# Attention over pooled keys followed by a gated feed-forward layer: scores of three batches as split products, four low parts on GpSimd, new orders

## The chip, the core and the metric

One core of a Trainium2 chip runs the whole program. The metric is the device time of one execution in microseconds (us). Of the kernel before, three runs were timed, and one execution was profiled.

## The reference

```python
def _attn_ref(q, k, v):                 # 8 batches, 8 heads, 576 rows, 64 columns
    k_p = k.reshape(B, H, 72, 8, D).mean(axis=3)
    v_p = v.reshape(B, H, 72, 8, D).mean(axis=3)
    scores = scale * np.matmul(q, k_p.transpose(0, 1, 3, 2))
    scores = scores - np.max(scores, axis=-1, keepdims=True)
    attn = np.exp(scores)
    attn = attn / (np.sum(attn, axis=-1, keepdims=True) + 1e-09)
    return np.matmul(attn, v_p)
def _moe_ref(x, w_in, w_out):           # x: 4608 x 512, w_in: 512 x 2048, w_out: 2048 x 512
    h = x @ w_in
    g = h * np.clip(h + 3.0, 0.0, 6.0) / 6.0
    return g @ w_out
```

Everything is float32. Where the kernel wants a product quickly, it splits each operand into a high part, rounded to fp32r, and a low part, the fp32r rest, and adds three fp32r products: high by high, high by low, low by high. A product of whole float32 operands is issued as one matmul, and the trace shows two records for it.

## The kernel before

The 4608 rows are cut into blocks (`BLOCKS`: 512, 256, and ten of 384). Blocks 0 to 3 go through the feed-forward layer one after the other, a step for each of the 16 slices `f` of the hidden width: `Step.h` (L1048), the gate (`relu` L1056, `gate` L1060), the split of g (`hi` L1064 on ScalarE, `lo` L1068 on VectorE) and `Step.out` (L1078). While block 0 runs, the weights of each slice are made ready by `Prep`: two passes of ScalarE, `join` (L972, VectorE), `hi` (L996, ScalarE) and `lo` (L1001, VectorE). Blocks 4 to 11 go in pairs through `super_block` and `out_seven`, where both matrix products are made of seven smaller ones: L1319, moving 384 columns, and L1401, moving 256. Their weights come back from DRAM in chunks of 512 KB (`chunk`, the DMA is L1208): a ring of `NSTREAM` = 7 buffers, 4 in one pool (`wsFalse`) and 3 in another (`wsTrue`). A chunk holds the weights of 12 matmuls of L1319 or 18 of L1401.

The attention of a later block runs between these matmuls. For every tile of 128 rows and each of two groups of four heads there is a score step: `Scores.product` (L686: two matmuls of a query tile, 128 x 128 and stationary, with the block-diagonal keys of a pair of heads, 144 moving columns, both whole float32), the maximum (L690), four exponentials (L695), the reciprocal (L711), and the division (L722, L728, mostly on GpSimd). A tile that lies in two batches takes twice as many matmuls. Then come transposes (L792, L794) and products with the values (`av`, L862; those of batch 1 and later are fp32r and move 192 or 384 columns). `prep_k` sums eight keys (L489) and writes them scaled into the key tile of the batch (L498); `load_q` brings a tile of q.

The order of the instructions on each engine is written out by hand as a table of numbers (`ORDER`), for PE, DVE, Activation and Pool and for SP's DMAs. Each engine's queue is strictly in that order.

Of the kernel before, what the change touches and what calls it, by code (L numbers as in the profile page):

```python
# [8 lines left out]
F32 = mybir.dt.float32  # L9
F32R = mybir.dt.float32r  # L10
# [7 lines left out]
P = 128  # L18
# [8 lines left out]
TLAG = 3  # L27

# [11 lines left out]
CHUNK, NSTREAM, NFIRST, NC, NREL = 2, 7, 4, 3, 2  # L40
# [19 lines left out]
        191 174 171 175 196-197 176-177 193-194 198 178-180 199 181 186 182 192 183 200 215 195 201 218 202-203 221  # L60
        204 219 224 205 208 225 222 226 206 227 207 228-229 220 234 209 235 216 236 217 237 254 243 255-256 238
        257-258 248 210 223 239 251 259-260 240 249-250 244 261 274 282 241 283 262 245 252 263 275 253 264-265 242
        284-286 276 279 268 280 269 287 270 281 303 271 288 272 304 289 305 294 309 273 306 290 310-311 291 312 307
        331 292 313 293 314 317-318 300 308 332 334 333 335 337 319 338 320 246 336 321 339-340 295 322 301 247 341
        362-363 342 296 302 326 357 323 365 324 358 366-369 327 364 343-345 325 346 266 370 328 351 347-348 371 359
        352 372 385-387 267 373 388-389 374 354 277 353 278 375 391-392 355 376 356 416 393-394 382 390 395 419 383
        396 384 417 400 377 409 420 401-402 378 422 379 403-404 410 423 405 411 406 424-427 297-299 407 428 418 441
        454-455 408 315 456-458 429 438 444 430 442 421 451 431-433 445-446 316 459 452 460-463 439 464-465 482 440
        349 483-484 453 485-489 443 490 466 329 491 330 479 492 350 493 360 473 476 380 361 467-468 480 381 397-399
        477 494 474-475 478 495 412 481 497 500 503 413-415 498-499 434 501 435-436 504 509 447 437 448 505 496 449  # L70
        502 450 510 530 544 469 511-512 531 470-471 536 521 506 537 472 515 513 545 516 532 514 533 546 562 522 517
        534-535 538-543 547 507 548 508 549 527 550-552 556 553 557 554 558-559 518 555 560 523 561 519-520 564 524
        565-566 528 567 525 578-580 526 581 568-569 529 582 575 583-586 570 587-588 576 600 577 601 589 571 602-605
        572 606 597 607 592 608-609 598 620-621 610-611 593 573 622 563 623 594 599 617-618 624-625 629-630 614
        631-632 643 633 644 574 634 590-591 615 645 616 646-648 637 651 619 652-653 595-596 666 654 640-642 655 638
# [270 lines left out]
def attention_moe_kernel(  # L346
# [63 lines left out]
    def ring(name):  # L410
        return pool.tile([P, S], F32, name=name, tag="ring", bufs=4)
# [681 lines left out]
    for t in kbds:  # L1093
        nc.gpsimd.memset(t, 0.0)
# [619 lines left out]
```

## Time and profile before

| what | value |
|---|---|
| median of 3 runs | 867.75 us (867.69 to 869.7) |
| the profiled execution | 867.65 us, of which the span of its instructions is 865.8 us |
| TensorE busy in the span | 857.1 us, 99% |
| VectorE busy | 671.9 us, 78% |
| ScalarE busy | 557.8 us, 64% |
| GpSimd busy | 96.6 us, 11% |
| granted TensorE clock | full throughout |

A record of a matmul lasts from its start to its modelled end, and these overlap: a record of 128x384 lasts 342 ns, and the next one starts some 174 ns later. So the price of a matmul is read from the distance of starts, over a run of them, and not from its duration. A caution on single distances: the record that follows a short matmul starts early, and its own distance to the next is longer by as much. Sums from one short matmul to the next one do not have this fault.

### The profile page before, as it was taken

The page shows a single profiled execution, that of the slowest core. Times are in us where ns is not written, and L with a number is a line of the kernel's source. Part 1 is how long each engine was busy: PE and PEld are TensorE (multiplying, and loading weights), DVE is VectorE, ACT ScalarE, POOL GpSimd, SP SyncE. Part 2 cuts the span into 40 slices and gives each one's busy share as a digit, 9 for nine tenths or more (in the row PEclk, how much of TensorE's full clock was granted, in tenths as well). Part 3 has the DMA queues.
Part 4 walks back from the last instruction along what each step waited for, and adds up shares of the span by engine and source line. Part 5 has one row for each costly group of instructions (what it writes and reads, how often), then busy time and mean ns, then how long its engine had stood idle before and what let it go on. Part 6 is the DMA issues. An engine that isn't in the chain of part 4 may idle for free.

```text
span 865.8 us, 16054 instructions
## 1 busy us (share of the span) xinstructions
PE 857.1 (99%) x5556; PEld 814.4 (94%) x5556; DVE 671.9 (78%) x1313; ACT 557.8 (64%) x1483; POOL 96.6 (11%) x188
## 2 busy tenths in 40 slices
PE   8999999999999999999999999999999999999998
PEld 8878889989889898999999999999999999999998
DVE  7989568887877678897998688899777697276764
ACT  5999648586657457677755677756785745255443
POOL 6210002030202002101101011201120000000000
PEclk9999999999999999999999999999999999999999
DMA  9981126455387778987787987878855788877874
GB/s 332 380 284 49 50 62 218 126 154 147 121 274 253 225 245 262 363 294 247 227 295 259 348 285 231 273 245 277 269 207 195 236 279 273 290 243 257 263 260 137
DMA packets 118095, 204.21 MB, mean 236 GB/s; under 512 B 13568, under 2 KB 72192, under 8 KB 118016
## 3 DMA queue, kind: packets, MB, share of 16 engines
q1 hardware_dynamic: 117872, 203.20, 70.9%
q8 instruction: 44, 0.72, 0.4%
q14 instruction: 35, 0.29, 0.1%
q10 hardware_dynamic: 144, 0.00, 0.0%
HBM read 164.37 MB, written 38.80 MB: 235 GB/s over the span
## 4 chain that ended last, share of the span: by engine, by line
PE 93%; DVE 3%; ACT 2%; issue 1%; DMA 0%; POOL 0%; SPq 0%; DVEq 0%; ACTq 0%
PE psx L1401 27%; PE psx L1319 26%; PE psh L1048 15%; PE pso L1078 15%; PE psa L862 4%; PE psa L686 4%; PE psa L792 2%; ACT e L695 1%; DMA stage<-k_l 0%; PE psa L794 0%; DVE sm L706 0%; DVE vst L606 0%; DVE mx L690 0%; POOL stage L580 0%; ACT r L1284 0%
## 5 line engine op out<-in xcount | busy, mean ns | idle before, releaser
L1319 PE MATMUL psx<-x,wsFalse 128*128 128x384 f32 x768 | 159.2, 342 | 0.0
L1048 PE MATMUL psh<-xhi,w 128*128 128x384 f32 (+2 forms) x520 | 157.4, 346 | 0.1
L1401 PE MATMUL psx<-wsFalse,part 128*128 128x256 f32 x1152 | 153.9, 283 | 0.0
L1401 PEld LDWEIGHTS psx<-wsFalse,part 128*128 128x128 f32 x1152 | 144.8, 189 | 0.0
L1078 PE MATMUL pso<-w,ghi 128*128 128x512 f32 x384 | 139.9, 403 | 0.0
L1303 ACT CAST part<-g 128x768 fp32r<-128x768 f32 x112 | 93.3, 836 | 65.7 <-PE psx L1401 60.3
L1319 PEld LDWEIGHTS psx<-x,wsFalse 128*128 128x128 f32 x768 | 133.5, 188 | 1.2 <-ACT c L1298 0.2
L1304 DVE TENSOR_TENSOR part<-g,part 128x768 fp32r<-128x768 f32 x112 | 107.5, 964 | 28.2 <-ACT part L1303 27.4
L1319 PE MATMUL psx<-x,wsTrue 128*128 128x384 f32 x576 | 124.8, 341 | 0.5 <-ACT c L1298 0.5
L1401 PE MATMUL psx<-wsTrue,part 128*128 128x256 f32 x864 | 117.1, 284 | 0.0
L1401 PEld LDWEIGHTS psx<-wsTrue,part 128*128 128x128 f32 x864 | 110.2, 191 | 0.0
L1048 PEld LDWEIGHTS psh<-xhi,w 128*128 128x128 f32 x520 | 94.9, 188 | 11.4 <-DVE g L1060 1.4
L1319 PEld LDWEIGHTS psx<-x,wsTrue 128*128 128x128 f32 x576 | 100.6, 188 | 1.2 <-ACT c L1298 1.1
L695 ACT ACTIVATE e<-psa,mx 128x72 f32<-128x72 f32 x256 | 80.3, 325 | 16.6 <-DVE mx L690 11.4
L1048 PE MATMUL psh<-xlo,w 128*128 128x384 f32 (+2 forms) x260 | 85.9, 342 | 0.0
L1298 ACT COPY c<-psx 128x384 f32<-128x384 f32 x96 | 45.8, 481 | 54.3 <-PE psx L1319 51.8
L1290 DVE TENSOR_TENSOR g<-psx,c 128x384 f32<-128x384 f32 x96 | 52.4, 555 | 36.6 <-PE psx L1319 21.3
L1078 PEld LDWEIGHTS pso<-w,ghi 128*128 128x128 f32 x384 | 70.9, 188 | 9.2 <-ACT ghi L1064 0.3
L1078 PE MATMUL pso<-w,glo 128*128 128x512 f32 x192 | 74.8, 400 | 0.0
L722 POOL TENSOR_TENSOR a<-e,sm 128x256 f32<-128x256 f32 x60 | 42.9, 716 | 239.9 <-DVE sm L711 188.8
L1284 ACT ACTIVATE r<-g,small 128x384 f32<-128x384 f32 x96 | 58.2, 618 | 15.5 <-DVE g L1290 12.6
L1285 DVE SCALAR_TENSOR_TENSOR g<-r,g 128x384 f32<-128x384 f32 x96 | 52.1, 558 | 11.7 <-ACT r L1284 11.4
(123 smaller groups left out, 1355.5 us busy)
## 6 DMA issues: line engine op xcount, KB each, us to landing
wsFalse<-wd SPq DMA_DIRECT2D x64, 512.0 KB, 4.9
wsTrue<-wd SPq DMA_DIRECT2D x48, 512.0 KB, 4.4
wsFalse<-w2t SPq DMA_DIRECT2D x40, 512.0 KB, 5.2
wsFalse<-w2d SPq DMA_DIRECT2D x24, 512.0 KB, 5.2
wsTrue<-w2d SPq DMA_DIRECT2D x24, 512.0 KB, 5.1
wsTrue<-w2t SPq DMA_DIRECT2D x24, 512.0 KB, 5.0
raw<-w_in_l SPq DMA_DIRECT2D x16, 512.0 KB, 9.3
raw<-w_out_l SPq DMA_DIRECT2D x16, 512.0 KB, 9.0
```

The costliest lines, as they stand in the source:

```text
L695: nc.scalar.activation(self.e[:, h], self.ps[:, h], AF.Exp, bias=self.mx[:, h : h + 1], **sums)
L722: engine.tensor_tensor(out=self.a[:, : 4 * D].rearrange("p (h s) -> p h s", h=4), in0=e[:, :, :D], in1=sm[:, :, None].broadcast_to([P, 4, D]),
L1048: nc.tensor.matmul(self.ps, l[f][:, c, :], r[:, c, :], start=c == 0 and i == 0, stop=c == NCC - 1 and i == 2)
L1078: nc.tensor.matmul(pos, l, r, start=f == 0 and i == 0, stop=f == NF - 1 and i == 2)
L1284: nc.scalar.activation(r, src, AF.Relu, bias=half_low, scale=GSCALE / (6.0 * WSCALE))
L1285: nc.vector.scalar_tensor_tensor(out=g_of[i][:, k], in0=r, scalar=GSCALE, in1=src, op0=ALU.min, op1=ALU.mult)
L1290: nc.vector.tensor_tensor(out=g_of[i][:, k], in0=ps, in1=kept, op=ALU.add)
L1298: nc.scalar.copy(c, ps)
L1303: nc.scalar.copy(t[:, 0], src)
L1304: nc.vector.tensor_tensor(out=t[:, 1], in0=src, in1=t[:, 0].bitcast(F32), op=ALU.subtract)
L1319: nc.tensor.matmul(ps, w[:, l, c * P : (c + 1) * P], t[:, r, c], start=o in (1, 2, 5) and c == 0 and k == 0, stop=c == 1 and k == 2, skip_ ...
L1401: nc.tensor.matmul(to, t[:, l, k, i * P : (i + 1) * P], w[:, k, r], start=begin and k == 0 and y == 0 and i % 2 == 0, stop=m == NM - 1 and ...
```

## The change

- The scores of batches 5 to 7 (`SPLIT_QK`). `split_q` makes a high part (ScalarE copy to fp32r) and a low part (VectorE subtraction) of the two query tiles of a score step; `prep_k` makes a low part of the keys besides the high one (VectorE). `score_sums` lists three fp32r products for each product that was one of whole float32: high q by high k, high q by low k, low q by high k.
- Key tiles are taken from a pool in turn and cleared by GpSimd for every batch. Before, two tiles were cleared once.
- `NSTREAM` goes from 7 to 6: 4 buffers in the one pool and 2 in the other.
- Four subtractions of block 0 move from VectorE to GpSimd: the low parts of the weights of slices 1 and 2 (128x1024) and the low parts of g of slices 1 and 3 (128x512).
- All five orders are written anew.

By count of the two programs, 60 score matmuls of whole float32 are replaced by 180 of fp32r, VectorE gains 30 subtractions of 128x256 and 24 of 64x72 and loses the four that moved, ScalarE gains 30 copies of 128x256, and GpSimd gains the four and eight clearings of 128x576.

```diff
+POOL_W, POOL_G = (1, 2), (1, 3)
+SPLIT_QK = 5
-CHUNK, NSTREAM, NFIRST, NC, NREL = 2, 7, 4, 3, 2
+CHUNK, NSTREAM, NFIRST, NC, NREL = 2, 6, 4, 3, 2
 ORDER = {
     "Pool": """
-        8 29 6 22 21 9 23 0 2-4 1 5 20 10-11 7 16 15 58 12 18 17 19 13 31 14 32 24-26 28 27 34 33 30 36 35 37-38 57
+        8 30 6 22 21 9 23 0 2-4 1 5 20 10-11 7 16 15 24 18 17 12 19 13 35 14 34 26 25 28 27 63 29 31-33 38 37 39-40
...
+    def keys_of(b):
+        if b not in kbds:
+            kbds[b] = pool.tile([P, NPAIR, 2 * SP], F32 if b < SPLIT_QK else F32R, name="kbd", bufs=2)
+            nc.gpsimd.memset(kbds[b].bitcast(F32), 0.0)
+        return kbds[b]
+
+    def low_keys(b):
+        if b % 2 not in klow:
+            klow[b % 2] = late[1].tile([P, NPAIR, 2 * SP], F32R, name=f"klo{b % 2}")
+            nc.gpsimd.memset(klow[b % 2].bitcast(F32), 0.0)
+        return klow[b % 2]
+
+    def split_q(tile, g):
+        for i, (b, _, _, _) in enumerate(tile):
+            if b < SPLIT_QK:
+                continue
+            if i and tile[0][0] >= SPLIT_QK:
+                x = ring("q2", F32R)[:, : NPAIR * P].rearrange("p (m c t) -> p m c t", m=2, c=2)
+            else:
+                x = late[1].tile([P, 2, 2, P], F32R, name="q2", bufs=1)
+            whole = qtiles[tile][i][:, 2 * g : 2 * g + 2]
+            nc.scalar.copy(x[:, 0], whole)
+            nc.vector.tensor_tensor(out=x[:, 1], in0=whole, in1=x[:, 0].bitcast(F32), op=ALU.subtract)
+            qparts[tile, i] = x
+
+    def score_sums(tile, p):
+        mms = []
+        for i, (qt, (b, _, _, _)) in enumerate(zip(qtiles[tile], tile)):
+            key = kbds[b][:, p]
+            if b < SPLIT_QK:
+                mms.append((qt[:, p], key))
+                continue
+            hi, lo = (qparts[tile, i][:, m, p % 2] for m in range(2))
+            mms += [(hi, key), (hi, klow[b % 2][:, p]), (lo, key)]
+        return mms
...
-                mul(kbds[b % 2][rows, p - i : p + 1, h * SP : (h + 1) * SP], ks[rows], scale)
+                at = rows, slice(p - i, p + 1), slice(h * SP, (h + 1) * SP)
+                to = keys_of(b)[at]
+                mul(to, ks[rows], scale)
+                if b >= SPLIT_QK:
+                    nc.vector.scalar_tensor_tensor(
+                        out=low_keys(b)[at],
...
-                for r, (qt, (b, _, _, _)) in enumerate(zip(qtiles[self.tile], self.tile)):
-                    nc.tensor.matmul(to, qt[:, p, :], kbds[b % 2][:, p, :], start=r == 0, stop=r == last)
+                mms = score_sums(self.tile, 2 * self.g + i)
+                for n, (l, r) in enumerate(mms):
+                    nc.tensor.matmul(to, l, r, start=n == 0, stop=n == len(mms) - 1)
...
-            nc.vector.tensor_tensor(
+            engine = nc.gpsimd if self.f in POOL_W else nc.vector
+            engine.tensor_tensor(
                 out=lo, in0=u.rearrange("p (i f) -> p i f", i=b - a), in1=hi.bitcast(F32), op=ALU.subtract
...
-            nc.vector.tensor_tensor(out=self.glo, in0=self.g, in1=self.ghi.bitcast(F32), op=ALU.subtract)
+            engine = nc.gpsimd if self.blk.j == 0 and self.f in POOL_G else nc.vector
+            engine.tensor_tensor(out=self.glo, in0=self.g, in1=self.ghi.bitcast(F32), op=ALU.subtract)
```

TensorE at a score step of batch 6, in the second pair of blocks. `psx` are sums of the feed-forward layer, `psa` a bank of the attention, `kbd` the keys, `qt` a tile of q. Before:

```order
L1319 MATMUL psx_6451<-x5_5648,wsFalse_6310 128x384 x6
L1319 MATMUL psx_6450<-x6_5698,wsFalse_6343 128x384 x6
L686 MATMUL psa_6514<-kbd0_83,qt_6117 128x144 x2
L1319 MATMUL psx_6354<-x4_5805,wsFalse_6343 128x384 x6
L1319 MATMUL psx_6451<-x3_5724,wsFalse_6364 128x384 x6
L1319 MATMUL psx_6548<-x1_5544,wsFalse_6364 128x384 x6
L686 MATMUL psa_6565<-kbd0_83,qt_6117 128x144 x2
```

and after, where `q2` is a split tile of q and `klo0` the low part of the keys:

```order
L776 MATMUL psa_6673<-kbd_6373,q2_6667 128x144
L1412 MATMUL psx_6548<-x7_5802,wsFalse_6515 128x384
L776 MATMUL psa_6673<-klo0_6376,q2_6667 128x144
L1412 MATMUL psx_6655<-x2_5614,wsFalse_6515 128x384
...
L776 MATMUL psa_6673<-kbd_6373,q2_6667 128x144 x2
L1412 MATMUL psx_6653<-x6_5742,wsFalse_6551 128x384
L1412 MATMUL psx_6548<-x4_5849,wsTrue_6571 128x384
L776 MATMUL psa_6673<-klo0_6376,q2_6667 128x144
L1412 MATMUL psx_6653<-x6_5742,wsFalse_6551 128x384
L776 MATMUL psa_6673<-kbd_6373,q2_6667 128x144
```

The two whole products of a step have become six, and they stand singly or in twos between matmuls of the feed-forward layer, not together.

VectorE in block 0, where the softmax of the last tiles (`stage_129`, with the sums `sm_326` and `sm_329`) meets the weights of slices 0 and 1 (`u`, `w_0_420`, `w_1_472`). Before:

```order
L711 RECIPROCAL sm_326<-sm_326 128x4
L972 SCALAR_TENSOR_TENSOR u_438<-raw_1_150,u_438 128x1024
L706 TENSOR_REDUCE sm_329<-stage_129 128x4
L1060 SCALAR_TENSOR_TENSOR g_397<-g_397,psh_377 128x256
L711 RECIPROCAL sm_329<-sm_329 128x4
L868 TENSOR_TENSOR xlo_337<-psa_428,xhi_336 128x256
L728 TENSOR_TENSOR stage_129<-stage_129,sm_329 128x96
L868 TENSOR_TENSOR xlo_337<-psa_433,xhi_336 128x256
L722 TENSOR_TENSOR stage_129<-stage_129,sm_329 128x256
L1001 TENSOR_TENSOR w_0_420<-u_283,w_0_420 128x512
L1001 TENSOR_TENSOR w_1_472<-u_438,w_1_472 128x2x512
L784 COPY a32_305<-psa_452 128x2x256
```

and after:

```order
L1063 SCALAR_TENSOR_TENSOR u_438<-raw_1_150,u_438 128x1024
L801 RECIPROCAL sm_326<-sm_326 128x4
L1093 TENSOR_TENSOR w_0_420<-u_283,w_0_420 128x512
L796 TENSOR_REDUCE sm_329<-stage_129 128x4
L959 TENSOR_TENSOR xlo_337<-psa_428,xhi_336 128x256
L801 RECIPROCAL sm_329<-sm_329 128x4
L959 TENSOR_TENSOR xlo_337<-psa_433,xhi_336 128x256
L812 TENSOR_TENSOR stage_129<-stage_129,sm_329 128x256
L818 TENSOR_TENSOR stage_129<-stage_129,sm_329 128x96
L1152 SCALAR_TENSOR_TENSOR g_397<-g_397,psh_377 128x256
L875 COPY a32_305<-psa_452 128x2x256
```

The reciprocal `sm_326` now stands behind the join of slice 1, a subtraction of 128x512 has come ahead of the last division and a gate has gone behind it, and the subtraction `w_1_472` is gone from VectorE.

GpSimd at the same place, before:

```order
L722 TENSOR_TENSOR stage_128<-stage_128,sm_320 128x256
L728 TENSOR_TENSOR stage_128<-stage_128,sm_320 128x96
L728 TENSOR_TENSOR stage_129<-stage_129,sm_326 128x96
L722 TENSOR_TENSOR stage_129<-stage_129,sm_326 128x256
L498 TENSOR_SCALAR kbd1_84<-ksum_654 64x72 x2
L467 MEMSET qt_505 128x4x64
```

and after:

```order
L818 TENSOR_TENSOR stage_129<-stage_129,sm_326 128x96
L812 TENSOR_TENSOR stage_129<-stage_129,sm_326 128x256
L688 MEMSET vlo_1986 128x512
L1093 TENSOR_TENSOR w_1_472<-u_438,w_1_472 128x2x512
L511 MEMSET qt_505 128x4x64
L1093 TENSOR_TENSOR w_2_571<-u_283,w_2_571 128x2x512
L1161 TENSOR_TENSOR glo_580<-g_574,ghi_578 128x512
L580 TENSOR_SCALAR kbd_85<-ksum_654 64x72 x2
```

Three of the four subtractions now stand behind the last division, ahead of the scaled keys of batch 1.

## Rows read from the trace of the kernel before

**Rows 1.** The page: busy time of the engines, the granted clock in 40 slices, and the chain that ended last by engine.

```profile
PE 857.1 (99%) x5556; PEld 814.4 (94%) x5556; DVE 671.9 (78%) x1313; ACT 557.8 (64%) x1483; POOL 96.6 (11%) x188
PEclk9999999999999999999999999999999999999999
PE 93%; DVE 3%; ACT 2%; issue 1%; DMA 0%; POOL 0%; SPq 0%; DVEq 0%; ACTq 0%
```

**Rows 2.** Busy time by stretch (from:to in us, its length, then busy us and instructions of PE, PEld, DVE, ACT and POOL, the granted clock, DMA share and GB/s).

```profile
8.00:28.00 20.00, 18.36 (x128) 16.44 (x127) 18.60 (x52) 15.79 (x41) 12.32 (x22) 1.00 1.04 387
45.00:340.00 295.00, 294.57 (x1598) 259.98 (x1597) 230.69 (x506) 202.50 (x597) 30.73 (x60) 1.00 0.54 175
340.00:480.00 140.00, 139.42 (x993) 138.03 (x992) 119.80 (x229) 94.68 (x261) 18.25 (x30) 1.00 0.83 280
550.00:600.00 50.00, 50.00 (x416) 49.93 (x415) 46.28 (x72) 36.02 (x89) 7.68 (x10) 1.00 0.79 256
600.00:620.00 20.00, 19.73 (x147) 19.37 (x146) 14.88 (x36) 11.26 (x44) 1.73 (x4) 1.00 0.91 292
```

**Rows 3.** The waits of PE in the first 45 us: who waited for whom, us in total, times, the longest.

```profile
PE idle L549 <- POOL ident masks.py:199: 2.4, 1, 2.4
PE psa L783 <- DVE stage L728: 0.7, 1, 0.7
PE psa L783 <- POOL stage L728: 0.4, 1, 0.4
PE psa L781 <- POOL stage L722: 0.3, 1, 0.3
```

**Rows 4.** PE in order of time (start, length, then line, operation, operands and count): a score step and three transposes among matmuls of 384 columns, and a run of the latter alone.

```profile
500.15 0.65 PE L686 MATMUL psa<-kbd,qt 128*128 128x144 f32 x4
500.55 4.44 PE L1319 MATMUL psx<-x,wsTrue 128*128 128x384 f32 x24
504.82 0.38 PE L792 MATMUL psa<-ident,a 128*128 128x128 f32 x2
505.04 0.27 PE L794 MATMUL psa<-ident,ar 128*128 128x128 f32 x1
505.07 2.34 PE L1319 MATMUL psx<-x,wsTrue 128*128 128x384 f32 x12
507.25 0.38 PE L792 MATMUL psa<-ident,a 128*128 128x128 f32 x2
...
521.41 3.31 PE L1319 MATMUL psx<-x,wsTrue 128*128 128x384 f32 x18
524.55 0.33 PE L862 MATMUL psa<-ahi,vhi 128*128 128x384 f32 x1
```

**Rows 5.** The same view: single fp32r products of 192 columns among those of 256, and a run of the latter.

```profile
440.43 0.25 PE L862 MATMUL psa<-ahi,vlo 128*128 128x192 f32 x1
440.51 0.90 PE L1401 MATMUL psx<-wsTrue,part 128*128 128x256 f32 x6
441.25 0.25 PE L862 MATMUL psa<-arem,vrem 96*128 96x192 f32 x1
441.34 1.13 PE L1401 MATMUL psx<-wsTrue,part 128*128 128x256 f32 x8
442.31 0.25 PE L862 MATMUL psa<-ahi,vhi 128*128 128x192 f32 x1
442.40 0.66 PE L1401 MATMUL psx<-wsTrue,part 128*128 128x256 f32 x4
442.90 0.25 PE L862 MATMUL psa<-alo,vhi 128*128 128x192 f32 x1
...
444.17 1.46 PE L1401 MATMUL psx<-wsFalse,part 128*128 128x256 f32 x11
445.47 0.26 PE L862 MATMUL psa<-arem,vrem 96*128 96x192 f32 x1
```

**Rows 6.** The score matmuls as a group: records, busy us, mean ns of one, idle before.

```profile
L686 PE MATMUL psa<-kbd,qt 128*128 128x144 f32 x288 | 53.6, 286 | 0.0
```

**Rows 7.** GpSimd and VectorE: durations (min/median/max ns) of one GpSimd operation of two inputs, then single instructions in order of time, two of GpSimd and one of VectorE.

```profile
L722 POOL TENSOR_TENSOR a<-e,sm x60: 607/613/1324, 136.7 to 643.1; 128x256 f32<-128x256 f32 x60
...
11.82 0.34 POOL L728 TENSOR_TENSOR stage<-stage,sm 128x96 f32<-128x96 f32 x1
...
24.87 1.18 POOL L728 TENSOR_TENSOR stage<-stage,sm 128x96 f32<-128x96 f32 x1 [4.47 <-DVE sm L711]
...
24.65 1.20 DVE L972 SCALAR_TENSOR_TENSOR u<-raw,u 128x1024 uint32<-128x1024 uint32 x1
```

**Rows 8.** Groups of VectorE by line: the two kinds of subtraction that move, and one of 128x256.

```profile
L804 DVE TENSOR_TENSOR alo<-psa,ahi 128x256 fp32r<-128x256 f32 x56 | 23.3, 417 | 6.6 <-ACT ahi L803 6.3
L1001 DVE TENSOR_TENSOR w<-u,w 128x1024 fp32r<-128x1024 f32 x14 | 17.0, 1219 | 0.0
L1068 DVE TENSOR_TENSOR glo<-g,ghi 128x512 fp32r<-128x512 f32 x15 | 10.3, 685 | 1.4 <-ACT ghi L1064 1.4
```

**Rows 9.** The weight chunks: from the page, one kind of issue with KB and us to landing; then waits of SP's DMA queue from 480 us on (us in total, times, the longest).

```profile
wsFalse<-w2d SPq DMA_DIRECT2D x24, 512.0 KB, 5.2
SPq L1208 <- PE psx L1319: 125.8, 63, 6.3
SPq L1384 <- DVE kept L1381: 11.6, 5, 5.9
```

More of the change, by code (lines that the diff above doesn't have):

```diff
@@ L60 @@
[L60 to L64, printed above, removed]
@@ new lines @@
+        4077-4078 4075 4079-4088 4097-4099 4109 4100-4103 4089 4104 4018-4019 4090-4091 4020-4021 4105 4022-4023
+        4076 4106-4108 4092 4115 4050 4110 4116 4111 4051-4055 4093 4112 4117 4094 4118-4119 4068 4120 4113
+        4069-4070 4121-4122 4114 4127-4129 4123 4130 4124-4125 4131 4095 4126 4133-4134 4096 4135 4132 4148 4136
+        4145 4137 4146 4138-4139 4147 4140 4149 4141 4150 4142-4144 4154 4196-4197 4151 4198 4152 4155 4153
+        4166-4167 4199 4156-4158 4172 4159-4160 4184 4168 4185 4173 4186 4300 4248 4174-4177 4301 4187 4249
@@ L341 @@
+        497 501 500 502 496 503-514 516 518-519 515 520 517 521 524 522-523 525-560 562-568 561 569-571 573 572
+        574-576 579 578 580 577 581-582
     """,
@@ L408, in const, with ring @@
         return consts[f >= NF // 2]
-    def ring(name):
-        return pool.tile([P, S], F32, name=name, tag="ring", bufs=4)
+    def ring(name, dtype=F32):
+        return pool.tile([P, S], dtype, name=name, tag="ring", bufs=4)
     def behind(ins, name):
@@ L497, in prep_k @@
                 mul = nc.scalar.mul if b > 1 else nc.gpsimd.tensor_scalar_mul
-                mul(kbds[b % 2][rows, p - i : p + 1, h * SP : (h + 1) * SP], ks[rows], scale)
+                at = rows, slice(p - i, p + 1), slice(h * SP, (h + 1) * SP)
[4 more added lines that the diff above has]
+                        out=low_keys(b)[at],
+                        in0=ks[rows],
+                        scalar=scale,
+                        in1=to.bitcast(F32),
+                        op0=ALU.mult,
+                        op1=ALU.subtract,
+                    )
     vraw = {}
@@ L680, in product @@
             ps = att_bank()
-            last = len(self.tile) - 1
             for i in range(2):
-                p = 2 * self.g + i
                 to = ps[:, 2 * SP * i : 2 * SP * (i + 1)]
-                for r, (qt, (b, _, _, _)) in enumerate(zip(qtiles[self.tile], self.tile)):
-                    nc.tensor.matmul(to, qt[:, p, :], kbds[b % 2][:, p, :], start=r == 0, stop=r == last)
+                mms = score_sums(self.tile, 2 * self.g + i)
+                for n, (l, r) in enumerate(mms):
+                    nc.tensor.matmul(to, l, r, start=n == 0, stop=n == len(mms) - 1)
             self.ps = ps[:, : 4 * SP].rearrange("p (h s) -> p h s", s=SP)
@@ L738, in scores @@
     def scores(j, tile, g):
+        split_q(tile, g)
         s = Scores(tile, g)
@@ L1091, in attention_moe_kernel @@
     nc.gpsimd.memset(half, 0.5)
-    kbds = [fixed.tile([P, NPAIR, 2 * SP], F32, name=f"kbd{i}") for i in range(2)]
-    for t in kbds:
-        nc.gpsimd.memset(t, 0.0)
+    kbds = {}
+    for b in range(2):
+        keys_of(b)
     nc.scalar.activation(half, half, AF.Exp)
```

585 lines of the change are left out of this document (312 added, 273 removed).

## The prediction

> **What bounds the kernel now.** I read the busy times of the page first: TensorE is busy for 857.1 of 865.8 us and holds 93% of the chain that ended last, at a full granted clock [rows 1]. The stretches and the waits then tell where the other 8.7 us lie. 2.4 us are the wait for the first identity tile [rows 3], 1.6 us lie between 8 and 28 us, 0.4 between 45 and 340, 0.6 between 340 and 480, 0.3 between 600 and 620 [rows 2], and what is left, some 3.4 us, is the start's remainder and the tail after the last matmul. So from 28 us to the tail nothing waits that an order could win back except about 1.3 us. The kernel's time there is the sum of what its matmuls cost, and the question is the price of a matmul, read from the distance of starts.
>
> **Price of a whole float32 score matmul.** 18 matmuls of 384 columns take from 521.41 to 524.55, 0.1744 us each. From the score step at 500.15 to the next short matmul at 504.82 are 4.67 us with 24 of them, 4.19 us; four records of the score step cost the rest, 0.48 us, 0.121 each [rows 4]. The program has 144 such matmuls where the trace has 288 records [rows 6], so one is two records, 0.242 us.
>
> **Price of a short fp32r product.** None of 144 columns is in the trace, but its neighbours on both sides are. Three transposes of 128 columns and 12 matmuls of 384 lie between 504.82 and 507.25: 2.43 - 12 x 0.1744 = 0.34 us, 0.112 each [rows 4]. Among matmuls of 256 columns, which cost (445.47 - 444.17)/11 = 0.118 us, three fp32r products of 192 columns take 442.90 - 440.43 - 18 x 0.118 = 0.35 us, 0.115 each, and they stand there singly, as the new score products do [rows 5]. So 256 columns cost 0.118, 192 cost 0.115, 128 cost 0.112: under 256 columns the price hardly falls. That is what it looks like when the load of the stationary tile, and not the streaming, sets the pace, since each of these loads 128 columns. I take 0.112 us for 144 columns, from the nearer row. From below the bound is streaming alone: 144/256 of 0.118, 0.066 us. From above it is 0.115.
>
> The Trainium skill, page "TensorE: Matmul & The Clock Gate", section "Back-to-back issue gap", gives about 81 ns for a matmul of 128 columns in a stream of loads and matmuls. By that figure 180 products would cost 14.6 us and the exchange would be even. The 0.112 us of the transposes is 38% above it, so the row is used.
>
> **The change on TensorE.** 60 whole products go: 60 x 0.242 = 14.5 us. 180 short ones come: 180 x 0.112 = 20.2 us. Three products in fp32r cost more than one of two records: 0.336 against 0.242. As TensorE does not wait in that part of the program, all of it lies on the path: **+5.7 us** (-2.6 if streaming alone counted, +6.2 at 0.115). That the products now stand singly changes nothing, since the single products of 192 columns paid the same.
>
> **Block 0.** VectorE is busy for 18.6 of the 20 us from 8 to 28 [rows 2], and TensorE waits there for the divisions, 0.7 + 0.4 + 0.3 us [rows 3]. The change takes two subtractions of 1.22 us and two of 0.69 from it [rows 8], 3.8 us. But in the order of before all four lie after these waits, and TensorE does not wait behind them. What counts is the order ahead of the last division. There a subtraction of 128x512 has come in front (about 0.6) and a gate of 128x256 has gone behind (about 0.35), so the division ends some 0.3 us later. In exchange, seven small TensorE matmuls stand ahead of it that stood behind, 5 x 0.118 + 2 x 0.112 = 0.8 us. That would win 0.5 us.
>
> Against it stands GpSimd. Its operation of 256 elements takes 0.613 us, of 96 elements 0.34 [rows 7], which makes 0.0017 us an element, so about 1.9 us for 1024 and 1.05 for 512, by my estimate. But the same operation of 96 elements took 1.18 us when VectorE ran a join of two inputs from 24.65 to 25.85: GpSimd stood still for about as long as the overlap lasted [rows 7]. In the new order a join stands on VectorE three rows behind the last division, so the subtraction of slice 1 on GpSimd, which can begin when ScalarE has made the high part at about 28.3, needs 1.9 us of its own and meets one stop of 1.2: about 31.5, where VectorE had it done by about 29.4. TensorE's third row of slice 1 waits for it, and the work that stands in front lasts until about 30.6 to 31.3. Queued behind this on GpSimd are the second slice and then the keys of batch 1. I take 0 us for the block. The bounds are -1.6 (every wait between 8 and 28 gone) and +2.0 (each of the four GpSimd operations waited for by 0.5).
>
> **Orders elsewhere.** They can win back at most the 1.3 us of idle time after 45 us. I take -0.3.
>
> **New waits.** The ring of chunks loses a buffer. A chunk lasts 12 x 0.1744 = 2.1 us on TensorE. The DMA queue waits for a buffer to come free (125.8 us behind L1319 alone), so loads start as early as buffers allow; six chunks ahead, 12.6 us, become five, 10.5 us. A load lands in 5.2 us [rows 9]. The margin of 5.3 covers this unless the queue is held up, and single waits for a result to store are up to 5.9 us [rows 9]: 0.6 us short, at five places or so. VectorE gains 30 subtractions at 0.42 [rows 8], 12.5 us, and 24 small ones on the keys at less than 0.42, so up to 22 us in all, ScalarE 30 copies, over some 150 us. Between 550 and 600 VectorE has 3.7 us free of 50 [rows 2]; a third of the added subtractions there would fill it. GpSimd's clearings hide behind its idle time (it is busy 11%, rows 1). I take +0.4; the bounds are 0 and +5.
>
> **The sum** is 5.7 + 0 - 0.3 + 0.4 = +5.8 us on the profiled execution's 867.65 (span 865.8, and 1.85 around it), 873.4 us. That execution lies 0.1 us below the median of the runs, 867.75, so the same holds against it.
>
> **Rivals.**
> - *Not slower: loads hide.* If, at 144 columns among long matmuls, the load goes beside the matmul ahead, a product costs 0.066 us and the step falls to 0.20 from 0.242: -2.6 us, 865.1. It decides from 0.080 us a product (14.5/180) downwards. Half hidden, at 0.089, it is +1.5, 869.2. The first would be what three passes against four mean on paper. Against it: the single products of 192 columns stood behind matmuls of 256 and 384 and still paid 0.115 [rows 5]. The skill's 81 ns lies at this turning point.
> - *The orders win back the idle time*, all of it after 8 us (2.9 us), and no new wait comes: 867.65 + 5.7 - 2.9 = 870.4. For it: all five orders were made anew. Against it: the last division is not earlier.
> - *New waits*: VectorE becomes the bound between 550 and 600, the ring runs dry behind held-up stores, GpSimd is late in block 0: +3 to +5 more, 876.5 to 878.5.
>
> That the change doesn't do what it says is no rival: the counts of the two programs show the exchange of 60 for 180.
>
> **How the numbers follow.** About 0.3%, 2.6 us, is what a measurement of this kernel can tell from no change, so slower begins at 870.3. My forecast, 871.3 to 876, has 0.60. Hidden loads have 0.11 (0.07 faster, 0.04 same). Won-back idle time has 0.12 (0.07 same, 0.05 slower). New waits have 0.12. Cases that I have not thought of have 0.05 (0.03 faster, 0.02 same). Slower is 0.60 + 0.05 + 0.12 = 0.77, same 0.13, faster 0.10. The range from 869.5 to 878 leaves out the hidden loads, the unknown cases and the far end of the waits, just under 0.2.
>
> **What would show it.** In the profile after, a stretch from one single score product of 144 columns to the next, less its long matmuls, should give 0.11 us a product; 0.066 would make the prediction wrong. TensorE should stay busy all through from 30 us on. The four GpSimd subtractions should last longer than 1.9 and 1.05 us, and TensorE's third product of slice 1 should come at about 31.5 us. Waits of L1412 or L1494 on a `ws` DMA, or on VectorE's `part` between 550 and 600, would show the third rival.

## The result and the profile after

| | median | runs | profiled span | TensorE busy | VectorE | ScalarE | GpSimd |
|---|---|---|---|---|---|---|---|
| before | 867.75 us (867.5 to 869.7) | 5 | 865.8 | 857.1 | 671.9 | 557.8 | 96.6 |
| after | 876.45 us (875.93 to 876.94) | 5 | 874.1 | 865.5 | 684.9 | 564.5 | 103.7 |

The medians lie 8.7 us apart, where 5.8 were forecast; the ratio of the runs is 1.0096, 95% interval [1.0082, 1.011]. The granted clock of TensorE was full in both profiled executions.

The page of after, busy time of TensorE and the chain that ended last, against [rows 1]:

```profile
PE 865.5 (99%) x5616; PEld 819.4 (94%) x5616; DVE 684.9 (78%) x1363; ACT 564.5 (65%) x1513; POOL 103.7 (12%) x200
PE 87%; DVE 7%; ACT 3%; DMA 1%; issue 1%; SPq 0%; DVEq 0%; ACTq 0%
```

TensorE is still the bound, but 6% of the span have gone from it in the chain, four of them to VectorE and one each to ScalarE and DMA. That is the first sign that more has happened than dearer matmuls.

**The price of a product.** TensorE of after in order of time, with single score products among matmuls of 384 columns, against [rows 4, 5]:

```profile
667.07 0.23 PE L776 MATMUL psa<-klo,q 128*128 128x144 f32 x1
667.14 0.38 PE L1412 MATMUL psx<-x,wsTrue 128*128 128x384 f32 x1
667.36 0.34 PE L1412 MATMUL psx<-x,wsFalse 128*128 128x384 f32 x1
667.53 0.23 PE L776 MATMUL psa<-kbd,q 128*128 128x144 f32 x1
```

From one single product to the next are 0.46 us, with two long matmuls between. Less 0.1744 for each of these, a short product costs 0.111 us. Over the 25 places of this trace where short products stand among matmuls of 384 columns alone the median is 0.111 as well. The exchange is therefore 180 x 0.111 - 60 x 0.242 = +5.5 us, as forecast.

**Where the rest lies.** For a table of lost time I took the start of a given feed-forward product (L1140, L1171, L1412, L1494, counted in order of start) and subtracted all matmuls that started ahead of it, each at the price of its kind (long ones of 384 columns 0.1744, of 256 0.118 us, of 512 0.233, short ones of up to 192 columns 0.111, records of whole float32 scores 0.121, and of whole float32 products of 256 columns with the values of batch 0 0.217). What is left is time in which TensorE did not start what it could have.

| lost up to the (us) | first product, at 20 us | 97th, at 51 us | 289th, at 96 us | 2401st, at 515 us | last |
|---|---|---|---|---|---|
| before | 5.6 | 7.9 | 7.6 | 11.5 | 14.5 |
| after | 6.5 | 8.9 | 9.1 | 13.2 | 17.7 |
| difference | 0.9 | 1.0 | 1.5 | 1.75 | 3.2 |

So 1.5 us are lost by 96 us, while block 0 runs, 0.2 more by 515 us, and 1.45 between there and the last matmul. With the exchange that makes 8.7 us between the last matmuls of the two kernels. The tail behind it became 0.3 us shorter, which leaves the 8.4 us between the spans; the profiled execution itself (875.93) was 0.5 below the median.

The waits of TensorE in after (who waited for whom, us in total, times, the longest):

```profile
PE psa L953 <- DVE arem L906: 0.6, 2, 0.3
PE psx L1494 <- DVE part L1397: 0.6, 1, 0.6
PE psa L883 <- ACT e L785: 0.3, 1, 0.3
PE psh L1140 <- ACT w L1087: 0.2, 1, 0.2
...
PE psa L874 <- DVE stage L818: 0.2, 1, 0.2
```

Of the waits for divisions, 0.7 + 0.4 + 0.3 us in [rows 3], the last row is what is left. The first row lies at 441.8 and 698.4 us, the second at 584.8, the fourth at 51.7, in block 0. No row names a `ws` chunk: the ring of six did not run dry.

The second wait is the largest. TensorE, and then VectorE, of after in order of time around it:

```profile
583.13 1.10 PE L1494 MATMUL psx<-wsFalse,part 128*128 128x256 f32 x8
584.79 0.51 PE L1494 MATMUL psx<-wsFalse,part 128*128 128x256 f32 x2 [0.55 <-DVE part L1397]
```

```profile
577.33 0.96 DVE L1397 TENSOR_TENSOR part<-g,part 128x768 fp32r<-128x768 f32 x1
578.21 0.95 DVE L1325 TENSOR_TENSOR x<-x,x 128x768 fp32r<-128x768 f32 x1
579.07 0.95 DVE L1451 TENSOR_TENSOR g<-g 128x768 f32<-128x768 f32 x1
579.94 0.95 DVE L1397 TENSOR_TENSOR part<-g,part 128x768 fp32r<-128x768 f32 x1
580.81 1.82 DVE L1451 TENSOR_TENSOR g<-g 128x768 f32<-128x768 f32 x2
582.64 0.23 DVE L582 SCALAR_TENSOR_TENSOR klo<-ksum,kbd 64x72 fp32r<-64x72 f32 x1
582.90 0.96 DVE L1451 TENSOR_TENSOR g<-g 128x768 f32<-128x768 f32 x1
583.78 0.95 DVE L1397 TENSOR_TENSOR part<-g,part 128x768 fp32r<-128x768 f32 x1
```

Each VectorE instruction starts as the one ahead ends, without a bracket that names a wait. The `part` that TensorE needs ends at 584.73, and TensorE goes on at 584.79. Here VectorE is the bound, and a low part of the keys (L582), which the change added, stands in the row. The row without a gap is longer than what is shown: it lasts from 566.1 to 587.1 us. In the kernel before, too, VectorE had no gap from 568.4 to 586.3 us.

**Block 0.** GpSimd of after in order of time, the four subtractions that moved to it (three of the four rows, the last of 128x512), and the third row group of slice 1 on TensorE:

```profile
28.79 2.39 POOL L1093 TENSOR_TENSOR w<-u,w 128x1024 fp32r<-128x1024 f32 x1 [0.43 <-DMA stage<-vr_l]
...
33.42 2.47 POOL L1093 TENSOR_TENSOR w<-u,w 128x1024 fp32r<-128x1024 f32 x1 [1.99 <-ACT w L1087]
...
40.56 1.35 POOL L1161 TENSOR_TENSOR glo<-g,ghi 128x512 fp32r<-128x512 f32 x1 [4.67 <-ACT ghi L1156]
```

```profile
31.22 0.60 PE L953 MATMUL psa<-arem,vrem 96*128 96x256 f32 x2
31.47 0.82 PE L1140 MATMUL psh<-xhi,w 128*128 128x512 f32 x2
```

They took 2.4 us where VectorE had needed 1.22, and 1.35 where it had needed 0.69 [rows 8]: more than the estimates of 1.9 and 1.05, as forecast. The third row group came at 31.47, where 31.5 was forecast, without a wait of its own.

So GpSimd is not what lost the 1.5 us. The lost time begins earlier. TensorE of before, from the first sums of the values (L569, products with the identity matrix that add up eight values each, and that start as the load of the values lands) to the first feed-forward product:

```profile
10.23 1.14 PE L569 MATMUL psa<-stage,ident 128*128 128x128 f32 x8
...
16.93 0.60 PE L862 MATMUL psa<-a,v 128*128 128x256 f32 x2
...
19.10 0.66 PE L686 MATMUL psa<-kbd,stage 128*128 128x144 f32 x4
...
19.85 0.47 PE L1048 MATMUL psh<-xhi,w 128*128 128x256 f32 x1
```

Between 16.93 and 19.10 lie ten records of whole float32 products of 256 columns and nothing else, 0.217 us each. The same stretch of after, with a wait for a division in it:

```profile
10.43 1.16 PE L660 MATMUL psa<-stage,ident 128*128 128x128 f32 x8
...
16.29 0.42 PE L874 MATMUL psa<-ident,stage 128*96 128x128 f32 x2 [0.19 <-DVE stage L818]
...
20.31 0.37 PE L1140 MATMUL psh<-xhi,w 128*128 128x256 f32 x1
...
51.69 0.50 PE L1140 MATMUL psh<-xhi,w 128*128 128x512 f32 x1 [0.24 <-ACT w L1087]
```

The stretch takes 9.62 us before and 9.88 after, with two of these records fewer in it (0.43 us): 0.7 lost. The load landed 0.2 later besides, which is less than the 0.5 by which two executions of one program differ here (e11). In the five profiled kernels with the order of before in this stretch (before, e3, e4, e8, e9) 0.0 to 0.5 us are lost in it, in the eight with the new one (after twice, e1, e2, e5, e6, e7, e10) 1.0 to 1.3, so these 0.7 us belong to the new order. The gap at 51.69 is worth 0.4: the matmul started 0.63 after the one ahead, at a price of 0.233.

### The profile page after: what moved, and what is told of

Same layout as the page of the kernel before. It is cut to its first block, busy times and chain, and to the rows that moved or that the text cites. A ratio compares the mean times of both kernels' runs of the same rounds, so it can differ in the third digit from the quotient of the medians.

```text
span 874.1 us, 16271 instructions
## 1 busy us (share of the span) xinstructions
PE 865.5 (99%) x5616; PEld 819.4 (94%) x5616; DVE 684.9 (78%) x1363; ACT 564.5 (65%) x1513; POOL 103.7 (12%) x200
## 4 chain that ended last, share of the span: by engine, by line
PE 87%; DVE 7%; ACT 3%; DMA 1%; issue 1%; SPq 0%; DVEq 0%; ACTq 0%
PE psx L1412 27%; PE psx L1494 24%; PE pso L1171 13%; PE psh L1140 13%; PE psa L776 4%; PE psa L953 4%; PE psa L883 1%; DVE part L1397 1%; DVE g L1451 1%; DMA stage<-v_l 1%; DVE arem L906 0%; ACT e L785 0%; DMA wsTrue<-wd 0%; DVE alo L895 0%; ACT u L1054 0%
## 5 line engine op out<-in xcount | busy, mean ns | idle before, releaser
L1412 PE MATMUL psx<-x,wsFalse 128*128 128x384 f32 x912 | 199.7, 342 | 0.0
L1494 PE MATMUL psx<-wsFalse,part 128*128 128x256 f32 x1332 | 189.1, 283 | 0.6 <-DVE part L1397 0.6
L1494 PEld LDWEIGHTS psx<-wsFalse,part 128*128 128x128 f32 x1332 | 173.6, 189 | 1.0 <-DVE part L1397 0.7
L1412 PEld LDWEIGHTS psx<-x,wsFalse 128*128 128x128 f32 x912 | 158.4, 188 | 2.0 <-DVE g L1383 0.7
L1140 PE MATMUL psh<-xhi,w 128*128 128x384 f32 (+2 forms) x520 | 151.4, 344 | 0.5 <-ACT w L1087 0.2
L1171 PE MATMUL pso<-w,ghi 128*128 128x512 f32 x384 | 134.9, 402 | 0.0
L1140 PEld LDWEIGHTS psh<-xhi,w 128*128 128x128 f32 x520 | 94.3, 188 | 12.6 <-DVE g L1152 1.6
L1494 PE MATMUL psx<-wsTrue,part 128*128 128x256 f32 x684 | 105.6, 284 | 0.1
L1412 PE MATMUL psx<-x,wsTrue 128*128 128x384 f32 x432 | 104.6, 345 | 0.0
L1494 PEld LDWEIGHTS psx<-wsTrue,part 128*128 128x128 f32 x684 | 93.8, 190 | 0.2 <-ACT part L1396 0.2
L1140 PE MATMUL psh<-xlo,w 128*128 128x384 f32 (+2 forms) x260 | 86.3, 343 | 0.0
L1171 PEld LDWEIGHTS pso<-w,ghi 128*128 128x128 f32 x384 | 70.5, 188 | 9.1 <-ACT ghi L1156 0.2
L1412 PEld LDWEIGHTS psx<-x,wsTrue 128*128 128x128 f32 x432 | 75.6, 189 | 1.0 <-DVE g L1378 0.3
L1171 PE MATMUL pso<-w,glo 128*128 128x512 f32 x192 | 74.0, 402 | 0.0
L1378 DVE SCALAR_TENSOR_TENSOR g<-r,g 128x384 f32<-128x384 f32 x96 | 53.0, 561 | 13.8 <-ACT r L1377 13.5
```

The lines of the kernel that those rows point to most:

```text
L1140: nc.tensor.matmul(self.ps, l[f][:, c, :], r[:, c, :], start=c == 0 and i == 0, stop=c == NCC - 1 and i == 2)
L1171: nc.tensor.matmul(pos, l, r, start=f == 0 and i == 0, stop=f == NF - 1 and i == 2)
L1378: nc.vector.scalar_tensor_tensor(out=g_of[i][:, k], in0=r, scalar=GSCALE, in1=src, op0=ALU.min, op1=ALU.mult)
L1412: nc.tensor.matmul(ps, w[:, l, c * P : (c + 1) * P], t[:, r, c], start=o in (1, 2, 5) and c == 0 and k == 0, stop=c == 1 and k == 2, skip_ ...
L1494: nc.tensor.matmul(to, t[:, l, k, i * P : (i + 1) * P], w[:, k, r], start=begin and k == 0 and y == 0 and i % 2 == 0, stop=m == NM - 1 and ...
```

## The experiments

The theory after the result: the exchange costs 5.5 us by the number of products, whatever their columns; block 0 costs 1.5, most of it by its new order; the rest is VectorE, which the split loaded. The rivals for the part above 5.5 us were GpSimd itself, the ring of six, and a start that merely differs from program to program. Each comparison is with the kernel before on the same chip.

**e1_whole: scores whole again, all else as changed.**

```diff
-SPLIT_QK = 5
+SPLIT_QK = 8
```

> The kernel after with every score product as one of whole float32 again (SPLIT_QK = 8; 60 whole products for 180 short ones, no split of q or keys); ring of six, the four low parts on GpSimd and all five orders as after. Theory A (price): the exchange costs what the starts show, 60 x 0.242 against 180 x 0.111, so 5.5 us go: 871.0. The 3.2 us that are left over the kernel before lie in block 0 (some 1.5) and in small waits after 60 us (some 1.7). Rival B (the small waits come from the added subtractions and copies, 22 us of VectorE's work and its single split tile of q): they go too, 869.3. Rival C (the loads of the short products hide, the loss is the orders'): 60 x 0.242 against 180 x 0.080 would be even, so about 876.

Measured: 870.06 us, ratio 1.0024 [1.0015, 1.0034]. The split is worth 876.45 - 870.06 = 6.4 us (6.65 when each is taken against the kernel before in its own job): 5.5 of price, and 0.9 that the table of lost time shows between 515 us and the end (3.55 lost there against 4.43). 2.0 us stay that the split does not explain.

**e2_two: one of the three products left out.** The product of high q by low keys is not computed, so 120 short products take the place of the 60.

```diff
-            mms += [(hi, key), (hi, klow[b % 2][:, p]), (lo, key)]
+            mms += [(hi, key), (lo, key)]
```

> The kernel after with the product of high q by low keys left out of the scores: 120 short products in place of 180, nothing else changed, so the scores of batches 5 to 7 lack one low part. Theory A, 0.111 us a product: 60 x 0.111 = 6.7 us less, 869.8. Rival, streaming alone, 0.066 us: 4.0 less, 872.5. If the small waits in that stretch are set by VectorE and not by TensorE's own work, TensorE arrives earlier at them and part of the gain is lost: 870.5 to 872.

Measured: 871.28 us, 1.0036 [1.0022, 1.0049]: 5.2 us less than the changed kernel, where 60 x 0.111 = 6.7 us of products went. 1.5 us came back elsewhere, 0.8 of it behind 515 us by the table of lost time; the wait on `part` was still there with 0.6 us, and the work of VectorE was unchanged.

**e5_half72: half the columns.** The product with the low keys moves 72 columns in place of 144, so half of it is not computed.

```diff
-            mms += [(hi, key), (hi, klow[b % 2][:, p]), (lo, key)]
+            mms += [(hi, key), (hi, klow[b % 2][:, p, :SP]), (lo, key)]
...
-                    nc.tensor.matmul(to, l, r, start=n == 0, stop=n == len(mms) - 1)
+                    nc.tensor.matmul(to[:, : r.shape[-1]], l, r, start=n == 0, stop=n == len(mms) - 1)
```

> The kernel after with the product of high q by low keys moving 72 columns in place of 144 (60 of the 180 short products; the low keys of one head of each pair are left out of the scores). Theory A (under 256 columns something other than streaming sets the price, the load of the stationary tile as I argued): nothing changes, 876.4 within 0.4. Rival (the price falls with the columns): streaming of 72 columns is 0.033 us, 60 of them 2.0 us less, 874.4.

Measured: 876.81 us, 1.0098 [1.0084, 1.0111], which is no change from 876.45. TensorE of this kernel at the place shown above for after:

```profile
668.72 0.20 PE L776 MATMUL psa<-klo,q 128*128 128x72 f32 x1
668.75 0.41 PE L1412 MATMUL psx<-x,wsTrue 128*128 128x384 f32 x1
669.00 0.34 PE L1412 MATMUL psx<-x,wsFalse 128*128 128x384 f32 x1
669.18 0.23 PE L776 MATMUL psa<-kbd,q 128*128 128x144 f32 x1
```

0.46 - 2 x 0.1744 = 0.111 us for a product of 72 columns, as for 144. Between these widths columns cost nothing and the product as such costs 0.11 us. The kernel before held a sign of it that the prediction did not use, products with only 64 columns:

```profile
104.47 0.33 PE L862 MATMUL psa<-a,vrem 96*128 96x64 f32 x2
104.61 0.47 PE L1048 MATMUL psh<-xhi,w 128*128 128x512 f32 x1
104.92 0.40 PE L1078 MATMUL pso<-w,ghi 128*128 128x512 f32 x1
```

Two records of 64 columns and one matmul of 512 (0.233) take 0.45 us, so each record costs 0.11.

**e4_pool_alone: only the move to GpSimd, on the kernel before.** The order of before stands.

```diff
+POOL_W, POOL_G = (1, 2), (1, 3)
...
-            nc.vector.tensor_tensor(
+            engine = nc.gpsimd if self.f in POOL_W else nc.vector
+            engine.tensor_tensor(
```

> The kernel before with the four subtractions of block 0 on GpSimd, at the places that they have there in the kernel after (the last one two scaled keys later), and nothing else changed: ring of seven, whole products, all other orders as before. Theory A (GpSimd is late: its 2.4 us instead of VectorE's 1.2 put the low part of slice 1 some 1.5 us later): 0.5 to 1.0 us slower than before, 868.3 to 868.8. Rival B (the loss of block 0 comes from the new order of VectorE and ScalarE there, and the move itself is free): 867.75 within 0.2. Rival C (the move relieves VectorE): 867.0 or less.

Measured: 870.66 us, 1.003 [1.0018, 1.0041]: 2.65 us more than before in that job (868.01), beyond the expectation. TensorE's waits in this kernel that name the moved work, and two of the subtractions on GpSimd:

```profile
PE psh L1043 <- POOL w L996: 1.4, 2, 0.7
PE pso L1074 <- POOL glo L1064: 0.3, 1, 0.3
```

```profile
35.67 2.39 POOL L996 TENSOR_TENSOR w<-u,w 128x1024 fp32r<-128x1024 f32 x1
42.29 1.89 POOL L1064 TENSOR_TENSOR glo<-g,ghi 128x512 fp32r<-128x512 f32 x1 [4.23 <-ACT ghi L1059]
```

So without a new order the move costs TensorE 1.7 us of direct waits and about one more behind them. In the table of lost time, 5.5 us lie between 20 and 96 us, against 2.0 in the kernel before.

**e6_dve_lows: the four subtractions back on VectorE, in the new order.**

```diff
-POOL_W, POOL_G = (1, 2), (1, 3)
+POOL_W, POOL_G = (), ()
```

> The kernel after with the four low parts of block 0 on VectorE again, the one of slice 1 behind the copy of the transposed weights, the others behind the gate of their slice or where they stood before; all else as after. Theory A (GpSimd's 2.4 us in place of 1.2 is what makes block 0 late, in this order as in the one of before, where the move alone cost 2.65 us): 1.0 to 1.9 us less than after, 874.6 to 875.4. Rival (the order of after was made around the move, and with four operations of 3.8 us more VectorE is what is late): no gain or up to 1.5 more, 876.4 to 878.

Measured: 878.02 us, 1.0115 [1.0101, 1.0129], 1.6 us above the changed kernel (1.1 above its repetition, e11, with intervals that overlap). Certain is that nothing is won back: in the new order GpSimd's slowness is hidden, and it isn't what block 0 lost.

**e3_back0: block 0 in the order of before**, subtractions on VectorE, joined to the new order at the end of the block.

```diff
-POOL_W, POOL_G = (1, 2), (1, 3)
+POOL_W, POOL_G = (), ()
```

(and the rows of the five orders up to the end of block 0).

> The kernel after with block 0 as it was before: the four subtractions on VectorE again, and the instructions of the first block in the order that they had before, on every engine; the rest in the order of after. Theory A: block 0 costs 1.0 to 1.5 us in the kernel after and the time is not made up later: 875.0 to 875.4. Rival: what block 0 loses is absorbed by slack behind it, or the seam costs as much: 876.4.

Measured: 888.98 us, 1.0238 [1.0221, 1.0255]. As a whole time it tells nothing, since the join opened waits between 109 and 134 us, where the split of the next block's x (L922, L923) came too late, and behind such waits TensorE's granted clock stood at its lower level, 1.2 GHz, for 3.4 us from 112.4 and for 6.8 us from 132.9:

```profile
PE psh L1131 <- DVE xlo L923: 3.4, 1, 3.4
PE psh L1131 <- ACT xhi L922: 2.7, 1, 2.7
```

Ahead of the join its profile does answer the question. Lost time from the first sums of the values to the 289th feed-forward product, at about 96 us, by the prices of the table above:

| block 0 | subtractions on VectorE | on GpSimd |
|---|---|---|
| order of before | 2.4 (before, e3, e8) | 5.7 (e4) |
| new order | 4.45 (e6) | 3.7 (after, e11), 3.7 to 4.5 with e1, e2, e5, e7, e10 |

With the rows of before, the split kernel loses in block 0 what the kernel before lost. So the 1.3 us between 2.4 and 3.7 belong to the order of block 0, the part behind 51 us included: from the 97th to the 289th product TensorE gains 0.3 on the prices in e3 as in the kernel before, and loses 0.2 in after.

**e9_back0b: the first half of block 0 in the order of before**, joined by small repairs instead of a cut at one point.

```diff
-POOL_W, POOL_G = (1, 2), (1, 3)
+POOL_W, POOL_G = (), ()
```

(and the rows of the orders up to about 50 us).

> The changed kernel with its four low parts of block 0 back on VectorE and the first half of block 0 back in the order of before; from there on the order of the change, joined without a seam. Theory (about 1.5 us of the loss arise up to 95 us and belong to the new order in block 0): 1.0 to 2.0 us less than the changed kernel, 874.5 to 875.5 us, and TensorE's work up to 95 us as early as in the kernel before, within 0.4 us. Rival (the order in block 0 costs nothing, the start merely differs from program to program): 876.0 to 877.0 us.

Measured: 880.88 us, 1.0149 [1.0135, 1.0163]. Again a join spoils the whole:

```profile
PE psh L1132 <- DVE g L1144: 3.4, 2, 3.2
```

That wait lies at 68 to 72 us. Ahead of it, at 51 us, this kernel had lost 8.7 us, the changed one in the same job 9.5 (e11). Of these 0.75 us, 0.7 lie in the stretch from the first sums of the values to the first feed-forward product, where it lost 0.5 and the changed one 1.2. The order of before wins some 0.7 us in the first 50 us, then. The 0.5 that the changed kernel loses behind 51 us could not be tried in this way; for them there is e3.

**e8_before6: the ring of six alone, on the kernel before**, with the loads shifted by a place in SP's order so that six buffers can hold them.

```diff
-CHUNK, NSTREAM, NFIRST, NC, NREL = 2, 7, 4, 3, 2
+CHUNK, NSTREAM, NFIRST, NC, NREL = 2, 6, 4, 3, 2
```

> The kernel before with a ring of six chunks in place of seven: each load of a chunk from the seventh on takes the place in SP's order of the load behind it, all else as before. Theory A (the margin of 5.3 us covers the landing of 5.2 but not SP's hold-ups): 0 to 0.4 us more than before, 868.2. Rival (the ring is what cost the kernel after, with whole products again, some 1.2 us behind block 0): 869.0 to 869.5.

Measured: 886.3 us, 1.0201 [1.0184, 1.0219], 18 us more than before, far beyond every expectation. Its waits of TensorE:

```profile
PE psx L1393 <- DMA wsTrue<-w2d: 5.6, 2, 4.5
PE psx L1393 <- DMA wsFalse<-w2t: 4.0, 1, 4.0
PE psx L1311 <- DMA wsTrue<-wd: 2.7, 3, 1.8
PE psx L1311 <- DMA wsFalse<-wd: 1.2, 1, 1.2
```

13.5 us of waits name a chunk, and not one does in after. In two of them the granted clock fell from 1.00 to its lower level, 1.2 GHz (the value behind POOL's):

```profile
406.90:410.30 3.40, 2.88 (x10) 2.91 (x11) 0.69 (x1) 0.00 (x0) 0.00 (x0) 0.51 0.94 332
434.20:441.00 6.80, 4.79 (x22) 4.82 (x23) 1.47 (x3) 0.95 (x3) 0.00 (x0) 0.50 0.73 265
```

TensorE was at work for 2.9 and 4.8 us of these stretches. If it did half as much there, that is some 3.8 us more, by my estimate, and with the waits 17 of the 19.2 us by which this profiled execution is longer than that of before. The ring of six runs dry in the order of before (as moved by the shift) and not in the new one. Whether the missing buffer or the shift makes the waits was not separated: seven buffers with the shifted loads were not run.

**e7_qlow_pool: the 30 low parts of q on GpSimd.**

```diff
-            nc.vector.tensor_tensor(out=x[:, 1], in0=whole, in1=x[:, 0].bitcast(F32), op=ALU.subtract)
+            nc.gpsimd.tensor_tensor(out=x[:, 1], in0=whole, in1=x[:, 0].bitcast(F32), op=ALU.subtract)
```

> The kernel after with the 30 subtractions that make the low part of q on GpSimd in place of VectorE, at the places where they were by time; all else as after. Theory A (VectorE's added 12.5 us set the small waits between 430 and 700, which the return to whole products took away, some 0.9 us): 875.5. Rival (the waits are those of the orders, or TensorE now waits for GpSimd, which needs some 0.6 us for such an operation against 0.42 and stands still beside VectorE's operations of two inputs): 876.4 to 878.

Measured: 878.13 us, 1.0114 [1.01, 1.0128], 1.7 us above the changed kernel, 1.25 above its repetition. The group on GpSimd, and TensorE's wait on `part`:

```profile
L537 POOL TENSOR_TENSOR q<-qt,q 128x256 fp32r<-128x256 f32 x30 | 26.2, 872 | 195.4 <-ACT q L536 163.1 <-DMA wsTrue<-wd 32.4
```

```profile
PE psx L1486 <- DVE part L1389: 0.8, 1, 0.8
```

A subtraction took 872 ns there, twice the 435 ns that the same one takes on VectorE in after (L545), and the wait on `part` did not go. To take work from VectorE in this way is no cure.

**e10_no_low: VectorE's added work left out.** The 30 low parts of q and the 24 of the keys are not computed; all 180 products stand.

```diff
-            nc.vector.tensor_tensor(out=x[:, 1], in0=whole, in1=x[:, 0].bitcast(F32), op=ALU.subtract)
...
-            hi, lo = (qparts[tile, i][:, m, p % 2] for m in range(2))
+            hi = lo = qparts[tile, i][:, 0, p % 2]
...
-                    nc.vector.scalar_tensor_tensor(
-                        out=low_keys(b)[at],
...
+                    low_keys(b)
```

> The changed kernel without VectorE's 30 subtractions for the low parts of q and its 24 for the low keys in batches 5 to 7; this leaves those low parts out of the computation (q's high part is multiplied in place of its low one, and the low keys stay zero), while all 180 short products, ScalarE's copies and the orders stand. Theory (VectorE's added work is the bound at 577 to 586 us and sets a part of the small waits from 440 us on): about 0.5 to 1.2 us less than the changed kernel, 875.2 to 876.0 us, and the wait of 0.7 us at 584.8 us gone. Rival (the waits come from the order and not from VectorE's load): 876.2 to 876.8 us. If the short products themselves were not the price, but the work that feeds them, it would fall to about 871 us.

Measured: 874.97 us, 1.0081 [1.0069, 1.0094], 1.5 us below 876.45 and 1.9 below its control. TensorE of this kernel at the place of the wait:

```profile
582.48 0.28 PE L1475 MATMUL psx<-wsFalse,part 128*128 128x256 f32 x1
582.60 0.34 PE L934 MATMUL psa<-alo,vhi 128*128 128x384 f32 x1
582.77 1.68 PE L1475 MATMUL psx<-wsFalse,part 128*128 128x256 f32 x10
584.29 0.34 PE L934 MATMUL psa<-arem,vrem 96*128 96x384 f32 x1
```

Ten matmuls in a row where after had eight, a wait, and two. Between 515 us and the end this kernel lost 3.2 us, the changed one 4.4 and its control 4.3, the kernel before 3.0.

**e11_after_again: the changed kernel once more**, the control of e9 and e10, without an edit.

> The changed kernel once more, as the control for the two others of this job. All theories: 876.4 us, within 0.5 us.

Measured: 876.88 us, 1.0106 [1.0091, 1.0122], 4 runs, 876.13 to 878.1. Its profile had lost 7.1 us at the first feed-forward product, the other one 6.5: two executions of one program differ by 0.5 us there, as the first sums of the values could start at 10.94 and 10.43 us, when their load had landed.

## Why the prediction was right in direction and 3 us short

The measured 876.45 lies inside the stated range, 869.5 to 878, but above the main forecast, 871.3 to 876, and at the near end of the rival *New waits* (876.5 to 878.5). Of the three parts of that rival only VectorE came; the other part of what was missing is block 0. These two errors point the same way, so no luck made them cancel.

| term | forecast | measured | from |
|---|---|---|---|
| exchange of products | +5.7 (0.112 each) | +5.5 (0.111 each) | distances of starts |
| block 0 | 0 (-1.6 to +2.0) | +1.5 | lost time up to 96 us |
| orders elsewhere, and new waits | -0.3 + 0.4 | +0.2 from 96 to 515 us, +1.45 behind | lost time |
| tail | 0 | -0.3 | spans |
| sum | +5.8 | +8.4 between spans, +8.7 between medians | |

**The exchange was right, and so was the reading that the width hardly counts.** The forecast took the price from products of 192 and transposes of 128 columns, since the price hardly fell with the width. The trace gives 0.111 where 0.112 was taken, e5 shows that half the columns change nothing, and e1 that 6.4 us go with the split, 5.5 of them price. The rival by which the loads hide (0.066 us, or 0.089) is refuted. That it is the load of the stationary tile which makes the 0.11 us, as the prediction argued, is not shown: no run changed the load, and three transposes whose stationary tile has 96 columns cost 0.107 us each (15.68 to 16.00 us in the kernel before).

The Trainium skill, page "TensorE: Matmul & The Clock Gate", section "Back-to-back issue gap", gives about 81 ns for a matmul of 128 columns, by which, as an estimate, the exchange would have been even. This trace does not agree: it shows 111 ns for products of 144 columns and 112 for transposes of 128.

**Block 0 was mis-sized: 0 in place of 1.5 us.** The step that failed set a gain of 0.5 us from matmuls brought forward against a late GpSimd. What was foreseen of GpSimd came, and TensorE did not wait for it. The waits for divisions shrank too. What was missed is that the order which does both starts block 0 later: 0.7 us between the first sums of the values and the first feed-forward product, at 10 to 20 us, a stretch from which the prediction took only the waits for divisions. 0.1 more go by 51 us, 0.5 behind (0.4 of it at 51.69, behind a high part that ScalarE made late), and 0.2 are the later load. The subtractions taken from VectorE gave nothing back, as the prediction said of them. e4 and e6 show both sides: the move alone in the old order costs 2.65 us, and in the new order taking it back wins nothing. The order hides the move, and costs 1.3 us of its own for that: with the old rows in block 0 (e3) these 1.3 us are gone. Why the new order needs the late start, and whether the wait at 51.69 must be, stays open, since both attempts to put the old rows back opened other waits further on.

**New waits were mis-sized: 0.4 in place of about 1.6 us.** The mechanism was named, with its place: VectorE as the bound between 550 and 600, because it had 3.7 us free there [rows 2]. It stood in the third rival, and the sum took 0.4 for all waits. VectorE gained 30 x 0.435 + 24 x 0.238 = 18.8 us. e10, which takes just these away, gets back 1.2 us of the 1.45 behind 515 us. The share of the stretch misled: 3.7 of 50 us free looked like slack, but none of it lay between 568.4 and 586.3 us, where the row of the kernel before had no gap already, and where the wait came.

**The ring was judged too lightly, and by luck without harm.** The prediction bounded a dry ring by a shortfall of 0.6 us at five places. e8 shows 13.5 us of waits on chunks in the order of before. What the prediction called orders elsewhere, worth at most 1.3 us of idle time, probably is what made six buffers enough; as the shift of the loads in e8 was not run with seven buffers, that is argued and not shown. What the smaller ring would cost is not told by any row of before.

**The orders won nothing back** beyond that: from 96 to 515 us 4.1 us were lost, before 3.9.

No kernel of these beat the one before. The nearest, e1, keeps the move and the ring and is 2.0 us slower.

## What to carry to other kernels

When TensorE is busy throughout, count its instructions before its columns: a product with a stationary load of its own cost the same 0.11 us at 64, 72 and 144 columns here (0.115 at 192), so three narrow split products lose to one of two records. Work that is added to an engine with 7% of a stretch free is not free; look for the stretch in which the engine's row has no gap, since work added there can make TensorE wait. And a new order, a smaller ring and a moved operation are to be priced together: here the ring alone (e8, with its loads shifted) and the move alone (e4) each cost more than in the company of the new order.

## What the hardware showed that was not expected

- A product of 72 columns costs TensorE as much as one of 144: 0.111 us both times. A record of 64 columns costs 0.11 us as well.
- GpSimd needs 2.4 us for the subtraction of 128x1024 elements that VectorE does in 1.22, and 872 ns for one of 128x256 that VectorE does in 435. The same subtraction of 128x512 took 1.35 us in one kernel and 1.89 in another.
- The landing of the load of the values moves the start: in two profiles of the same program the first sums of the values started at 10.43 and 10.94 us, and the rest followed 0.5 us later. Distances within the start can be compared between kernels, moments can not.
